# Linear attention and a gated feed-forward: batch 0's k by two queues, batch 1 in nine-token layout, batch 2's x copied by VectorE

## The chip, the core and the metric

The kernel runs on one core of a Trainium2 chip. A core has a matrix engine (TensorE, PE in the profile, with its weight loads as PEld), a vector engine (VectorE, DVE), an engine for activation functions (ScalarE, ACT), GpSimd (POOL) and SyncE (SP). Each works through its own queue of instructions in program order and waits on semaphores for the others. Matmul results go to PSUM, everything else lies in SBUF; transfers to and from memory run on 16 DMA engines and are started from the queues of POOL, SP or ACT. The metric is the time of one execution in microseconds, lower is better.

## What is computed

Eight batches of 576 tokens with 8 heads of 64 values go through linear attention with the feature map elu(x) + 1, and the result, as 4608 tokens of 512 values, through a feed-forward with a gated activation:

```python
def phi(x):
    return np.where(x > 0, x, np.exp(x) - 1.0) + 1.0
q_p, k_p = (phi(q), phi(k))
kv = np.einsum('bhsd,bhse->bhde', k_p, v)
z = np.sum(k_p, axis=2)
num = np.einsum('bhsd,bhde->bhse', q_p, kv)
den = np.einsum('bhsd,bhd->bhs', q_p, z)[..., None] + 1e-06
...
h = x @ w_in                                # 512 -> 2048
g = h * (1.0 / (1.0 + np.exp(-beta * h)))
return (g @ w_out).astype(np.float32)       # 2048 -> 512
```

## The kernel before, in words

**Stages.** For each batch the kernel computes phi of k and q, the product of k and v (`kv_mm`, with a column of ones beside v that gives z), the transposed q, the numerator and denominator (`num_mm`), their quotient x (`num_norm`), x transposed (`x_trans`), then h (`h_phase`, line 453, 64 matmuls of 512 columns) with the Silu on ACT (line 445), and y (`y_mm`, line 505, again 64 matmuls). The order is written out by hand: the attention of batch b+1 is woven between the matmuls of h and y of batch b through a plan, which says after which group of matmuls which pieces are issued. Every engine keeps exactly this order. The main work takes 512 tokens of each batch; the last 64 tokens of every batch (the "tail") are gathered in `xT_tail` and go through h and y together at the end.

**Two layouts of tokens.** Batches 1 to 7 put four tokens on each of 128 partitions and the 64 tail tokens in a fifth slot on half of the partitions; a load is one DMA of 1024 packets and one of 512 for the tail (lines 71 to 79). The unused half of the fifth slot has to be cleared by memsets (`clear_tail`, line 92). Batch 0 has a layout of its own: nine tokens on each of 64 partitions, with heads 0 to 3 on the lower half and heads 4 to 7 on the upper half (`nine`, `load_nine`, lines 117 to 138). It has no unused half and no tail load. Its token order follows it through to the stores of y (`store`, line 484 onwards).

**Start.** While batch 0's k, q and v come in, PE runs warm-up matmuls (`warm`, line 575). All loads of inputs go through POOL's queue, which casts fp32 to bf16 on the way: k, part of q, v in two parts, the rest of q, w_in, then half of w_out, k and q of batch 1. No more than eight of its DMAs are seen outstanding: POOL waits for the landing of an older one before it issues the next. beta, 8 KB, is issued by SP (line 147), turned by a matmul (`beta_trans`, line 193), and made ready by five small DVE operations (`make_beta`, lines 199 to 205). exp runs on ACT (line 256), max(x,0)+1 on DVE ("relu", line 264), and phi is the minimum of both (line 270). For batch 0 the matmuls for z and those for v are separate (`kv_mm0`, line 307), as v comes last.

**Batch 1** is prepared during h and y of batch 0: exp at line 229, relu at 237, phi at 242, the copy of v into `vaug` beside its ones (`v_copy`, line 370), then inside `y_phase_wide(0, ...)` the 40 matmuls of `kv_mm` (line 344), their four copies out of PSUM into `kv_bd` (line 355), the scaling of w_out by 1/beta (`w_out_scale`, line 212), 16 transposes of q (line 380), and `num_mm` (399) with `num_norm` (413 to 415) for one tile of 128 tokens after another. Matmul results of attention use two double banks of PSUM (`att_banks`), which take turns.

**Batch 2** has its q transposed by a DMA (line 388), and its x by PE (`x_trans`, line 433), with the copy out of PSUM on ACT (line 372) inside `y_phase_wide(1, ...)`.

Of the kernel before, what the change touches and what calls it, by code (L numbers as in the profile page):

```python
# [16 lines left out]
def kernel(  # L17
# [99 lines left out]
    def nine(a, spec):  # L117

        names = " ".join(spec)
        flat = a.rearrange("p a b c -> p (a b c)")  # L120
        size = {"h": HH, "j": N9, "d": D}
        n = size["h"] * size["j"] * size["d"]
        return flat[:, 0:n].rearrange(f"p ({names}) -> p {names}", **size)

    q9 = nine(xqk[0][:, 0], "hjd")
    k9 = nine(xqk[0][:, 1], "hjd")
    v9 = nine(vraw[0], "hjd")

    def load_nine(dst, src, h0=0, h1=HH, j0=0, j1=N9):
        for g in range(2):  # L130
            nc.gpsimd.dma_start(  # L131
                out=dst[g * TAIL : (g + 1) * TAIL, h0:h1, j0:j1, :].rearrange(
                    "p h j d -> p h (j d)"
                ),
                in_=src[0, g * HH + h0 : g * HH + h1, :, :]
                .rearrange("h (p j) d -> p h j d", j=N9)[:, :, j0:j1, :]
                .rearrange("p h j d -> p h (j d)"),
            )
# [5 lines left out]
    clear_tail(1)  # L144
    nc.vector.memset(vraw[1][TAIL:P, :, NJ, :], 0.0)
    beta_row = consts.tile([FC, P], F32)
    nc.sync.dma_start(out=beta_row, in_=moe_beta.rearrange("(c p) -> c p", p=P))
# [3 lines left out]
    load_nine(k9, k)  # L151
    load_nine(q9, q, j1=4)
    make_identity(nc, identity)
    make_identity(nc, ident16)
    load_nine(v9, v, j1=6)
    load_nine(v9, v, j0=6)
    load_nine(q9, q, j0=4)
# [4 lines left out]
    load_k(1)  # L162
    load_q(1)
# [15 lines left out]
    for i in range(2):  # L179
        set_ones(i)  # L180
# [67 lines left out]
    x0 = {0: q9, 1: k9}  # L248
# [4 lines left out]
    def exp0(a, j0, j1):  # L253
        if j0 == 0:
            st["e0", a] = work9("e", bufs=3)
        nc.scalar.activation(  # L256
            st["e0", a][:, j0:j1].rearrange("p j h d -> p h j d"), x0[a][:, :, j0:j1],
            ACTF.Exp,
        )

    def relu0(a, j0, j1):
        if j0 == 0:
            st["r0", a] = work9("r")
        nc.vector.tensor_scalar(
            st["r0", a][:, j0:j1].rearrange("p j h d -> p h j d"), x0[a][:, :, j0:j1],
            0.0, 1.0, ALU.max, ALU.add,
        )

    def phi0(a, j0, j1):
        nc.vector.tensor_tensor(  # L270
            st["p0"][a][:, j0:j1], st["r0", a][:, j0:j1], st["e0", a][:, j0:j1], ALU.min
        )

    def q_trans0(t, banks, c0):


        for jj in range(2 if t < NJ else 1):
            for a in range(2):
                for g in range(2):
                    gs = slice(g * TAIL, (g + 1) * TAIL)  # L280
                    m0 = c0 + a * P + jj * TAIL
                    nc.tensor.matmul(
                        banks[:, g, m0 : m0 + TAIL],
                        st["p0"][0][gs, 2 * t + jj, 2 * a : 2 * a + 2, :],
                        identity[gs, gs],
                        is_transpose=True, start=True, stop=True, skip_group_check=True,
                    )

    def q_out0(t, banks, c0, dve):
        n = rows(t)  # L290
        src = banks[:, :, c0 : c0 + 2 * P].rearrange("p g (a n) -> p g a n", a=2)
        dst = st[0, "qT"][:, t].rearrange("p (g a) n -> p g a n", g=2)
        copy(dst[:, :, :, :n], src[:, :, :, :n], dve)
# [5 lines left out]
    def kv_mm0(kvp, j0, j1, of_v):  # L299


        for j in range(j0, j1):
            for a in range(2):
                for g in range(2):
                    gs = slice(g * TAIL, (g + 1) * TAIL)
                    cols = kv_cols(kvp, g, a)
                    nc.tensor.matmul(
                        cols[:, :, 0:D] if of_v else cols[:, :, D],
                        st["p0"][1][gs, j, 2 * a : 2 * a + 2, :],
                        v9[gs, 2 * a : 2 * a + 2, j, :] if of_v else ones[gs],  # L310
                        start=(j == 0 and a == 0 and not of_v),
                        stop=(j == N9 - 1 and a == 1 and of_v),
                        skip_group_check=True,
                    )

    def kv_evac0(kvp):
        for g in range(2):
            for i in range(2):
                gs = slice(i * D, (i + 1) * D)
                copy(  # L320
                    kv_bd[0][g][gs, :, i, :],
                    kvp[g][gs, 0 : 4 * (D + 1)].rearrange(
                        "p (a i e) -> p a i e", a=2, i=2
                    )[:, :, i, :],
                    g == 0,
                )

# [153 lines left out]
    out0 = out[0:S, :].rearrange("(p j) m -> p j m", j=N9)  # L481

    def tail_rows(b):
        if b == 0:
            return out0[:, N9 - 1, :]
        return out[b * S + MAIN : (b + 1) * S, :]

    def store(b, t, y_sb):
        if b < B:
            if b == 0:  # L490
                for i in range(2):
                    nc.sync.dma_start(
                        out=out0[:, 2 * t + i, :], in_=y_sb[i * TAIL : (i + 1) * TAIL, :]
# [89 lines left out]
    def F(f, *a, **k):  # L583
        return lambda: f(*a, **k)

    begin(0)
    st["warm"] = mm_bank([P, 512])
    warm(10)
    beta_trans()
    make_beta()  # L590
    warm(20)
    st["p0"] = [
        nine(st[0, "p"][:, a].rearrange("p j (h d) -> p j h d", h=H), "jhd")
        for a in range(2)
    ]
    exp0(1, 0, 5)
    exp0(1, 5, N9)
    exp0(0, 0, 4)
    relu0(1, 0, 5)
    relu0(1, 5, N9)  # L600
    phi0(1, 0, 5)
    relu0(0, 0, 4)
    phi0(1, 5, N9)
    phi0(0, 0, 4)
# [3 lines left out]
    q_trans0(0, qb, 0)  # L608
    q_trans0(1, qb, 256)
    q_out0(0, qb, 0, False)  # L610
    q_out0(1, qb, 256, False)
    kv_mm0(kvp, 0, 6, True)
    kv_mm0(kvp, 6, N9, True)
    kv_evac0(kvp)
# [4 lines left out]
    exp0(0, 4, N9)  # L619
    relu0(0, 4, N9)  # L620
    silu_table()
    num_norm(0, 0)
    phi0(0, 4, 6)
# [3 lines left out]
    q_trans0(2, qb2, 0)  # L627
    q_out0(2, qb2, 0, False)
    num_norm(0, 1)
    phi0(0, 6, N9)  # L630
# [3 lines left out]
    load_v(1)  # L634
    load_w_out(3)

    def tidy0():
        clear_tail(0)
        nc.vector.memset(vraw[0][TAIL:P, :, NJ, :], 0.0)

    def q_rest0():
        q_trans0(3, qb2, 256)
        q_trans0(4, qb2, 512)
        q_out0(3, qb2, 256, False)
        q_out0(4, qb2, 512, False)
# [11 lines left out]
            9: [F(x_trans, 0, 3), F(tidy0)],  # L657
# [9 lines left out]
    begin(1)  # L667
    exp_(1, 1)
    exp_(1, 0)
    silu_table()  # L670
    relu(1, 1)
    relu(1, 0)
    w_out_scale(2)
    phi(1, 1)
    v_copy(1)
    phi(1, 0)
    y_phase_wide(0, {
        4: [F(load_next, 3)],
        9: [F(kv_mm, 1), F(kv_evac, 1), F(w_out_scale, 3)],
        10: [F(q_trans, 1, 0, 1, wide=True), F(q_trans, 1, 2, 3, wide=True)],  # L680
# [3 lines left out]
        14: [F(num_mm, 1, 3), F(num_norm, 1, 3), F(q_trans, 1, 4, wide=True)],  # L684
# [24 lines left out]
        12: [F(num_mm, 2, 1), F(num_norm, 2, 1), F(x_trans, 2, 0, wide=True)],  # L709
        13: [F(num_mm, 2, 2), F(num_norm, 2, 2), F(x_trans, 2, 1, wide=True)],  # L710
        14: [F(num_mm, 2, 3), F(num_norm, 2, 3)],
# [64 lines left out]
```

## Time and profile before

| | us |
|---|---|
| median of 8 runs (lowest, highest) | 296.24 (296.04, 297.16) |
| the profiled execution, as timed | 296.14 |
| its span, first to last instruction | 294.4 |
| PE busy | 285.6 (97%) |
| ACT busy | 175.1 (59%) |
| DVE busy | 123.8 (42%) |
| POOL busy | 53.1 (18%) |
| mean granted clock of TensorE | 0.998 |

How to read it: a row of the profile's timeline gives start, duration, engine, line of the kernel, operation, what it writes and reads with the shape, how many instructions are merged in it, and in brackets how long the engine stood idle before it and what released it. PE's busy time includes pipelined ends and the warm-up, so 97% does not say that PE works at its peak. The costliest groups are the matmuls of y (line 505, 128.2 us in 560 instructions) and of h (line 453, 108.1 us in 560, and 14.0 us for the tails); ACT's largest is the Silu (97.4 us). POOL's queue moved 20.45 MB in 38912 packets, the queues of SP and ACT 16.20 MB in 33216.

### The profile page before, as it was taken

To read this page: it belongs to the slowest core of one execution; us is meant where nothing else is said; L and a number is where in the kernel's file an instruction comes from. 1 tells how busy PE (TensorE), PEld (TensorE's weight loads), DVE (VectorE), ACT (ScalarE), POOL (GpSimd) and SP (SyncE) were. 2 spreads that over 40 slices of the span, in tenths; PEclk is the share of its full clock that TensorE was granted. 3 is DMA by queue.
4 is the path that set the end of the run, shared out by engine and by line. 5 is a ranking of instruction groups with operands and counts; after the bars stand their busy time and mean duration, and the time that the engine had idled before them with its cause. 6 is when DMAs were issued, how large, how long until landed. Compare 5 with 4: busy or idle time off the path is not lost.

```text
span 294.4 us, 4771 instructions
## 1 busy us (share of the span) xinstructions
PE 285.6 (97%) x1912; PEld 143.9 (49%) x1912; DVE 123.8 (42%) x261; ACT 175.1 (59%) x234; POOL 53.1 (18%) x72
## 2 busy tenths in 40 slices
PE   8979999999899999999999999999999999999994
PEld 2567445644465544454444544454445444444444
DVE  5675488504375264517461646164715400110012
ACT  2799776889988771878077808790770077018500
POOL 8924475540004200320032000000000000000000
PEclk9999999999999999999999999999999999999999
DMA  7999999999538993799369955023502400120032
GB/s 109 196 204 344 260 274 191 257 193 190 86 143 108 177 133 117 125 176 144 98 134 166 157 101 125 2 77 111 127 0 72 118 36 0 38 94 13 0 74 71
DMA packets 72310, 37.09 MB, mean 126 GB/s; under 512 B 40912, under 2 KB 66784, under 8 KB 72288
## 3 DMA queue, kind: packets, MB, share of 16 engines
q0 software_dynamic: 38912, 20.45, 47.9%
q1 hardware_dynamic: 33216, 16.20, 23.6%
q8 instruction: 15, 0.25, 0.3%
q10 hardware_dynamic: 160, 0.13, 0.2%
q14 instruction: 7, 0.06, 0.0%
HBM read 36.71 MB, written 9.44 MB: 157 GB/s over the span
## 4 chain that ended last, share of the span: by engine, by line
PE 77%; DMA 11%; ACT 4%; issue 3%; POOL 2%; DVE 1%; ACTq 0%; POOLq 0%; DVEq 0%
PE mm L453 37%; PE mm L505 34%; DMA vraw<-in_v_dram 6%; DMA xT<-in_moe_w_out_dram 5%; PE att L399 3%; ACT e L229 2%; PE att L344 1%; PE mm L537 1%; POOL xqk L131 1%; ACT L229 1%; ACT g L445 1%; DVE qk_p L242 1%; POOL xqk L111 0%; PE mm L433 0%; ACT L445 0%
## 5 line engine op out<-in xcount | busy, mean ns | idle before, releaser
L445 ACT ACTIVATE g<-mm,beta_c 128x512 bf16<-128x512 f32 (+2 forms) x156 | 97.4, 634 | 87.8 <-PE mm L453 87.5
L505 PE MATMUL mm<-w_out,g 128*128 128x512 bf16 x560 | 128.2, 379 | 0.0
L453 PE MATMUL mm<-xT,w_in 128*128 128x512 bf16 (+2 forms) x560 | 108.1, 349 | 0.8 <-DMA w_in<-in_moe_w_in_dram 0.5
L453 PEld LDWEIGHTS <-w_in 128*128 128x128 bf16 x656 | 62.0, 98 | 61.7 <-DMA w_in<-in_moe_w_in_dram 0.6
L505 PEld LDWEIGHTS <-g 128*128 128x128 bf16 x560 | 52.9, 98 | 58.3
L515 DVE COPY y_sb<-mm 128x512 f32<-128x512 f32 x27 | 18.7, 692 | 70.5 <-PE mm L505 69.1
L229 ACT ACTIVATE e<-xqk 128x2560 bf16<-128x2560 bf16 x14 | 31.9, 2329 | 0.1
L415 DVE TENSOR_TENSOR xs<-att,rden 128x512 bf16<-128x512 f32 (+1 forms) x40 | 27.6, 689 | 1.4
L242 DVE TENSOR_TENSOR qk_p<-r,e 128x2560 bf16<-128x2560 bf16 x14 | 20.9, 1490 | 13.1 <-ACT e L229 12.4
L72 POOL DMA_DIRECT2D vraw<-in_v_dram x7 | 7.0, 995 | 84.2 <-DVE vaug L370 78.4
L355 DVE CAST kv_bd<-att 64x130 bf16<-64x130 f32 x28 | 8.2, 292 | 32.2 <-PE att L344 31.8
L413 DVE TENSOR_SCALAR den<-att 128x8 f32<-128x8 f32 (+1 forms) x40 | 6.5, 162 | 31.4 <-PE att L399 31.3
L399 PEld LDWEIGHTS <-q_pT 128*128 128x128 bf16 (+1 forms) x160 | 11.6, 100 | 11.0 <-DVE xs L415 2.4
L399 PE MATMUL att<-kv_bd,q_pT 128*128 128x130 bf16 (+1 forms) x160 | 15.8, 221 | 1.1 <-DMA q_pT<-qk_p 0.7
L453 PE MATMUL mm<-xT_tail,w_in 128*128 128x512 bf16 x64 | 14.0, 379 | 0.0
L237 DVE TENSOR_SCALAR r<-xqk 128x2560 bf16<-128x2560 bf16 x14 | 11.6, 836 | 3.6 <-DMA xqk<-in_q_dram 2.2
L575 PE MATMUL mm<-g 128*128 128x512 bf16 x35 | 10.5, 457 | 1.2 <-DVE g L143 1.2
L72 POOL DMA_DIRECT2D xqk<-in_k_dram x7 | 9.4, 1336 | 5.7 <-DMA w_in<-in_moe_w_in_dram 2.2
L229 ACT ACT_TABLE_LOAD x7 | 9.0, 1283 | 0.1
L414 DVE RECIPROCAL rden<-den 128x8 f32<-128x8 f32 (+1 forms) x40 | 8.1, 202 | 1.4
L256 ACT ACTIVATE e<-xqk 128x1280 bf16<-128x1280 bf16 (+1 forms) x4 | 4.4, 1155 | 5.4 <-DMA xqk<-in_k_dram 4.6
L72 POOL DMA_DIRECT2D xqk<-in_q_dram x7 | 6.3, 894 | 5.5 <-ACT q_pT L372 1.9
(71 smaller groups left out, 138.5 us busy)
## 6 DMA issues: line engine op xcount, KB each, us to landing
out_dram<-y_sb SPq DMA_DIRECT2D x28, 256.0 KB, 2.3
xqk<-in_k_dram POOLq DMA_DIRECT2D x7, 512.0 KB, 10.7
xqk<-in_q_dram POOLq DMA_DIRECT2D x7, 512.0 KB, 11.6
vraw<-in_v_dram POOLq DMA_DIRECT2D x7, 512.0 KB, 11.3
w_in<-in_moe_w_in_dram POOLq DMA_DIRECT2D x4, 512.0 KB, 10.8
g<-in_moe_w_out_dram POOLq DMA_DIRECT2D x4, 512.0 KB, 10.9
out_dram<-y_sb SPq DMA_DIRECT2D x14, 128.0 KB, 5.2
xqk<-in_moe_w_out_dram POOLq DMA_DIRECT2D x2, 512.0 KB, 13.9
```

The lines of the kernel that those rows point to most:

```text
L72: eng.dma_start(out=dst[:, :, 0:NJ, :].rearrange("p h j d -> p h (j d)"), in_=src[b, :, 0:MAIN, :].rearrange("h (p j) d -> p h (j d)", j=NJ),)
L229: nc.scalar.activation(st[b, "e", a][:, h0:h1], xqk[b % NX][:, a, h0:h1], ACTF.Exp)
L237: nc.vector.tensor_scalar(st[b, "r", a][:, h0:h1], xqk[b % NX][:, a, h0:h1], 0.0, 1.0, ALU.max, ALU.add)
L242: nc.vector.tensor_tensor(st[b, "p"][:, a].rearrange("p j (h d) -> p h j d", h=H)[:, h0:h1], st[b, "r", a][:, h0:h1], st[b, "e", a][:, h0: ...
L355: nc.vector.tensor_copy(kv_bd[b % 2][i][gs, :, g, :], st[b, "kvp"][gs, 2 * i : 2 * i + 2, :])
L399: nc.tensor.matmul(nps[:n, p // 2, c0 : c0 + 2 * (D + 1)], st[b, "qT"][:, t, p, :n], kv_bd[b % 2][p // 2][:, p % 2], start=True, stop=True ...
L415: nc.vector.tensor_mul(xs[:n], nv[:, :, :, 0:D], rden[:n, :, :, None].to_broadcast([n, 2, 4, D]))
L445: nc.scalar.activation(g_sb[b % 2][:, ff, c0:c1], hp[:, c0:c1], ACTF.Silu, scale=beta_c[:, ff : ff + 1],)
L453: nc.tensor.matmul(hp[:, c0:c1], w_in_sb[ff // 4][:, kc, (ff % 4) * P : (ff % 4 + 1) * P], x[:, t0:t1, kc, :] if b < B else x[:, kc, c0:c1 ...
L505: nc.tensor.matmul(yp, g_sb[b % 2][:, ff, t * P : (t + 1) * P], w_out_sb[ff // 4][:, ff % 4, :], start=(ff == 0), stop=(ff == FC - 1),)
L515: nc.vector.tensor_copy(y_sb, yp)
L575: nc.tensor.matmul(st["warm"], g_sb[0][:, FC - 1, 0:P], g_sb[0][:, FC - 1, :], start=True, stop=True, skip_group_check=True,)
```

## The change

It touches three places.

1. **Start.** The last four of the nine token slots of batch 0's k (`k_last`) are no longer loaded by POOL as bf16 but by SP as fp32, into memory of `g_sb[1]` that is free then; POOL loads the first five. beta's load moves from SP to ACT's queue. `make_beta` moves behind batch 0's first phi operations, and the warm-up after `beta_trans` has 15 matmuls for 20. The copies of the first two transposed q tiles become one. The clearing of batch 1's tail leaves the start.
2. **Batch 1** takes the nine-token layout: its k, q and v are two DMAs each of 256 packets; exp, relu, phi and the copy of v use the layout's functions, now with a batch as argument (`exp9`, `relu9`, `phi9`, `q_trans9`, `q_out9`, `kv_evac9`). The product of k and v takes 36 matmuls on half of the rows each (`kv_mm9`), the transposed q 32 + 4 small ones. As later batches use the same buffers in the old layout, the halves of the fifth slot are cleared after batch 1's phi (`tidy(1)`), and the ones of `vaug` are set after its kv (`set_ones(1)`). Its stores follow the token order: two per tile, not one.
3. **Batch 2**: the copies of the first two x tiles out of PSUM are made by DVE, and the second of them comes one step later in the plan.

```diff
+    x9 = [[nine(xqk[b][:, a], "hjd") for a in range(2)] for b in range(2)]
+    v9 = [nine(vraw[b], "hjd") for b in range(2)]
+    va9 = nine(vaug[1], "jhd", EA)
+    QF = 4
+    KF = 5
+    k_last = g_f[:, 0 : HH * (N9 - KF) * D].rearrange(
+        "p (h j d) -> p h j d", h=HH, j=N9 - KF
+    )
+
+    def load_nine(dst, src, b, j0=0, j1=N9, eng=nc.gpsimd):
         for g in range(2):
+            eng.dma_start(
+                out=dst[g * TAIL : (g + 1) * TAIL].rearrange("p h j d -> p h (j d)"),
+                in_=src[b, g * HH : (g + 1) * HH, :, :]
...
-    clear_tail(1)
-    nc.vector.memset(vraw[1][TAIL:P, :, NJ, :], 0.0)
+    load_nine(k_last, k, 0, KF, N9, eng=nc.sync)
     beta_row = consts.tile([FC, P], F32)
-    nc.sync.dma_start(out=beta_row, in_=moe_beta.rearrange("(c p) -> c p", p=P))
+    nc.scalar.dma_start(out=beta_row, in_=moe_beta.rearrange("(c p) -> c p", p=P))
...
-    load_nine(k9, k)
-    load_nine(q9, q, j1=4)
+    load_nine(x9[0][1][:, :, 0:KF], k, 0, 0, KF)
+    load_nine(x9[0][0][:, :, 0:QF], q, 0, 0, QF)
...
-    load_k(1)
-    load_q(1)
+    load_nine(x9[1][1], k, 1)
+    load_nine(x9[1][0], q, 1)
...
-    for i in range(2):
-        set_ones(i)
+    set_ones(0)
+    nc.vector.memset(va9[:, :, :, D : D + 2], 1.0)
...
+    def in9(b, a, j0, j1):
+        if b == 0 and a == 1 and j0 >= KF:
+            return k_last[:, :, j0 - KF : j1 - KF]
+        return x9[b][a][:, :, j0:j1]
...
+    def kv_mm9(kvp):
+
+        for a in range(2):
+            for j in range(N9):
+                for g in range(2):
+                    gs = slice(g * TAIL, (g + 1) * TAIL)
+                    nc.tensor.matmul(
+                        kv_cols(kvp, g, a),
+                        st[1, "p9"][1][gs, j, 2 * a : 2 * a + 2, :],
+                        va9[gs, j, 2 * a : 2 * a + 2, 0 : D + 1],
+                        start=(j == 0), stop=(j == N9 - 1), skip_group_check=True,
+                    )
...
+    def v_copy9():
+        nc.vector.tensor_copy(
+            va9[:, :, :, 0:D].rearrange("p j h d -> p h j d"), v9[1]
+        )
...
     beta_trans()
+    warm(15)
+    exp9(0, 1, 0, KF)
+    exp9(0, 1, KF, N9)
+    exp9(0, 0, 0, QF)
+    relu9(0, 1, 0, KF)
+    relu9(0, 1, KF, N9)
+    phi9(0, 1, 0, KF)
+    relu9(0, 0, 0, QF)
+    phi9(0, 1, KF, N9)
+    phi9(0, 0, 0, QF)
     make_beta()
-    warm(20)
...
-    q_out0(0, qb, 0, False)
-    q_out0(1, qb, 256, False)
+    q_out9(0, 0, 2, qb, 0, False)
...
-    load_v(1)
+    load_nine(v9[1], v, 1)
...
-    phi(1, 1)
-    v_copy(1)
-    phi(1, 0)
+    phi9(1, 1)
+    v_copy9()
+    phi9(1, 0)
+    tidy(1)
+
+    def kv1():
+        kvp = att_banks()
+        kv_mm9([kvp[:, 0], kvp[:, 1]])
+        kv_evac9(1, [kvp[:, 0], kvp[:, 1]])
+        set_ones(1)
+
+    def q1():
+        qb = att_banks(BF16)
+        for t in range(NJ):
+            q_trans9(1, t, qb, 256 * t)
+        q_out9(1, 0, 1, qb, 0, False)
+        q_out9(1, 1, 2, qb, 256, False)
+        q_out9(1, 2, 4, qb, 512, False)
...
-        9: [F(kv_mm, 1), F(kv_evac, 1), F(w_out_scale, 3)],
-        10: [F(q_trans, 1, 0, 1, wide=True), F(q_trans, 1, 2, 3, wide=True)],
+        9: [F(kv1), F(w_out_scale, 3)],
+        10: [F(q1)],
...
-        12: [F(num_mm, 2, 1), F(num_norm, 2, 1), F(x_trans, 2, 0, wide=True)],
-        13: [F(num_mm, 2, 2), F(num_norm, 2, 2), F(x_trans, 2, 1, wide=True)],
-        14: [F(num_mm, 2, 3), F(num_norm, 2, 3)],
+        12: [F(num_mm, 2, 1), F(num_norm, 2, 1), F(x_trans, 2, 0, wide=True, dve=True)],
+        13: [F(num_mm, 2, 2), F(num_norm, 2, 2)],
+        14: [
+            F(x_trans, 2, 1, wide=True, dve=True), F(num_mm, 2, 3), F(num_norm, 2, 3),
+        ],
```

## The prediction

> **What bounds the kernel now.** I read the page's slices first, then the chain of waits, then short windows, then the timeline at the three places that the change touches.
>
> ```profile
> PE   8979999999899999999999999999999999999994
> DMA  7999999999538993799369955023502400120032
> GB/s 109 196 204 344 260 274 191 257 193 190 86 143 108 177 133 117 125 176 144 98 134 166 157 101 125 2 77 111 127 0 72 118 36 0 38 94 13 0 74 71
> ```
>
> TensorE (PE) is busy nearly everywhere, but until the first h matmul it only warms up. The DMA row is full for ten slices (to 73 us). So two things can shorten the run: an earlier first h matmul, or fewer holes in PE afterwards. In the chain:
>
> ```profile
> 5.31 5.68 DMA vraw<-in_v_dram
> ...
> 30.04 11.52 DMA vraw<-in_v_dram
> ...
> 45.05 0.62 PE att L380 x8
> ```
>
> The start hangs on batch 0's loads, and the stage of batch 1 on its v. After 82.4 us the chain is PE alone, so a hole saved or made before then reaches the end in full.
>
> **A. Start: k by two queues.** The windows (us, busy time per engine, clock, DMA share, GB/s written) show where the DMAs stand idle:
>
> ```profile
> 1.50:2.00 0.50, 0.50 (x2) 0.15 (x1) 0.50 (x2) 0.50 (x1) 0.50 (x2) 1.00 0.06 14
> 2.25:2.50 0.25, 0.25 (x3) 0.01 (x1) 0.25 (x2) 0.00 (x0) 0.25 (x1) 1.00 0.00 0
> 2.75:3.00 0.25, 0.25 (x2) 0.09 (x1) 0.25 (x2) 0.00 (x0) 0.25 (x1) 1.00 0.93 74
> 3.75:4.00 0.25, 0.25 (x2) 0.15 (x1) 0.12 (x2) 0.00 (x0) 0.25 (x2) 1.00 1.29 217
> ```
>
> From 3.5 us they write some 195 GB/s, which is 390 GB/s of fp32 read. Before 2.55 us nothing flows but beta's 8 KB, at 1.5 to 2.0 us, though SP issued it at 0.75. And what ends the start is this:
>
> ```profile
> 13.90 0.58 DVE L264 TENSOR_SCALAR r<-xqk 128x1280 bf16<-128x1280 bf16 x1 [0.77 <-DMA xqk<-in_q_dram]
> 14.51 0.17 DVE L413 TENSOR_SCALAR den<-att 128x8 f32<-128x8 f32 x1
> ...
> 16.78 1.07 PE L453 MATMUL mm<-xT,w_in 128*128 128x128 bf16 x16 [0.46 <-DMA w_in<-in_moe_w_in_dram]
> ```
>
> VectorE (DVE) holds the first normalisation behind relu of q's rest, which waits for its DMA until 13.90; PE waits for w_in until 16.78. Both lie behind k and v in one first-in-first-out stream, so k's own earlier arrival gains nothing there: what counts is how much of the stream's bytes moves before POOL's loads flow. k_last is 4/9 of k's 1.18 MB, 0.52 MB. SP has nothing else to issue until 48.29, so k_last can flow from 1.6 us (as beta did). A 128-packet store occupies SP for 0.96 us and a 64-packet one for 0.68, so some 5 ns a packet; 2 x 256 packets take 2.6 us, about 200 GB/s. From 1.6 to 2.55 that is 0.19 MB, and in the ramp to 3.5 (where POOL's loads use under half of 390) 0.19 MB more: 0.38 MB / 390 GB/s = 1.0 us. Bounds: 0.3 (the packets come slower, or the ramp is the memory's) and 1.3 (all of k_last). **I take 0.8 us**, since the page's smaller stores land slowly in traffic (5.2 us for 128 KB).
>
> [...]
>
> The rest keeps pace. k(0:5) is only 0.65 MB of POOL's stream, so exp begins near 5.7 rather than 6.88; DVE then runs relu 0.58, relu of fp32 (0.48 as bf16 up to 0.97, twice the 512-element fp32 row of L212), phi 0.83, relu 0.47, phi 0.7 and 0.7: done by about 10. make_beta's five operations (1.1 us) now stand behind them and before kv_evac, which cannot come before v (10.99 - 0.8) plus its 36 matmuls (11.12 to 12.46, 1.34 us), so they are hidden; beta_c is first read at 17.21. Five warm matmuls fewer (5 x 0.216) end PE's warm-up at 9.1, before it is wanted. The merged q copy (1.02 against 2 x 0.55) ends before kv_evac. The two memsets of batch 1 taken out (0.48 + 0.27) lay where DVE idles later anyway (3.96 to 5.93).
>
> beta now goes by ScalarE (ACT), behind its table load: issue at 2.24, not 0.75. Alone it landed in 1.7 us (3.9); in traffic, by the 128 KB stores, up to 5.2 (7.5). PE asks at 5.6 and must then run 15 warm matmuls. At 7.5 the v part of kv would start at 11.7 and den at 14.3 instead of 13.7: +0.6. With 16 packets it is nearest to its own row: 0.
>
> **B. Batch 1 in nine-token layout.** The stage before:
>
> ```profile
> 41.65 0.83 DVE L370 COPY vaug<-vraw 128x2560 bf16<-128x2560 bf16 x1 [0.41 <-DMA vraw<-in_v_dram]
> 42.53 0.82 PE L344 MATMUL att<-vaug,qk_p 128*64 128x65 bf16 x40
> 45.05 0.62 PE L380 MATMUL att<-identity,qk_p 128*128 128x128 bf16 x8 [0.28 <-DVE kv_bd L355]
> 46.80 0.17 DVE L413 TENSOR_SCALAR den<-att 128x8 f32<-128x8 f32 x1
> 47.99 0.40 PE L433 MATMUL att<-identity,xs 128*128 128x128 bf16 x4
> ```
>
> PE: 40 kv matmuls took 0.76 (42.53 to 43.29); 36 of batch 0's kind take 1.34: +0.58. The 16 transposes of q took 1.35 (44.16 to 45.51) with their wait for a bank behind kv_evac; 32 small ones, by batch 0's 16 in 0.23, take 0.5, and the new bank use has no such wait: -0.85. PE alone would gain 0.3. But x_trans at 47.99 is released by DVE, and DVE's queue from v's landing is a straight line: before, v_copy 0.83, phi 1.49, evac 1.2, w_out_scale 1.67 and gaps, 5.15 from 41.65 to 46.80. After: v_copy 0.75 and phi 1.34 (9/10 each), **tidy 0.75** (memsets of 0.48 and 0.27), evac 1.2, **ones 0.19**, scale 1.67, gaps 0.1: 6.0. That is +0.85. Behind tidy wait kv_evac, w_out_scale(3) and every norm, and PE waits for those.
>
> Against it v lands sooner against PE: 3 x 512 packets for 3 x 1536. Loads with tails wrote 187 to 195 GB/s at 58 to 74 us; whole nine-token rows 196 to 210 at 4.0 to 5.5. 5% of 9.3 us (1.77 MB at 190) is 0.45; I take 0.3, as batch 0's smaller pieces ran at 188. **B = +0.5 us**, from +0.1 (DMA gives 0.7, and DVE's 0.41 idle is used) to +0.9 (gives nothing). exp gets shorter (2.33 to 2.1, twice), relu longer (0.83 to about 1.0); neither is last. Batch 1's stores are eight SP issues (5.48 for batch 0) for four (3.85); the last starts near 86, and SP's next work, a transpose, at 89.26. Two new orders have room: w_out(2) goes into k_last's place, but was issued at 25.68, long after k's relu; v(3) waits for tidy, but was issued at 50.13.
>
> **C. Batch 2.**
>
> ```profile
> 78.96 0.40 PE L399 MATMUL att<-kv_bd,q_pT 128*128 128x130 bf16 x4 [0.67 <-DMA q_pT<-qk_p]
> 81.74 0.59 ACT L372 ACTIVATE xT<-att 128x512 bf16<-128x512 bf16 x1
> 82.38 0.38 PE L433 MATMUL att<-identity,xs 128*128 128x128 bf16 x4 [0.29 <-ACT xT L372]
> ```
>
> The second x_trans waits for the first one's copy to leave its bank: PE stands from 81.91 to 82.38, 0.46. By DVE the copy (0.42) follows xs at 81.63, ends at 82.05, and x_trans now comes after four more y matmuls, at 82.78: no wait. But num(2,3) then meets a bank whose norm, pushed behind the copy, ends at 83.2: a hole of 0.2. h would start at 84.36, not 84.55: **-0.2** (from +0.2, if DVE's added 2 x 0.42 delays the norms more, to -0.46).
>
> The 0.67 hole before is a DMA transpose issued at 69.61 among loads that fill the DMAs until about 76. The loads end sooner by A and by B's packets (1.1), while PE is ahead by only 0.3 there. **-0.4**, between 0 and -0.67.
>
> **Sum:** -0.8 + 0.5 - 0.2 - 0.4 = -0.9 us. The profiled execution took 296.14 (span 294.4 and 1.7 around it), which makes 295.2; the median of all runs is 296.24, so 295.3.
>
> **Rivals.**
> - *The transfer is hidden anyway.* [...] Against: the empty windows. -0.2 + 0.6 (less help for v) - 0.3 = +0.1: 296.3. Chance 0.25.
> - *DVE's queue in batch 1 becomes the bound* (slower). tidy and ones put 0.94 ahead of the norms; PE's longer kv matmuls hold kv_evac too. It decides once v lands less than 0.2 sooner against PE: B = +0.9, the transposed q gains nothing, and a start of only -0.2: +0.7, 296.9. For: every instruction from v to den is back to back. Against: 0.41 of idle before v_copy. Chance 0.15.
> - *All covers hold*: k_last wholly hidden (-1.1), v early (+0.1), hole at 78.96 closed (-0.67), copies -0.3: -2.0, 294.3. Chance 0.12.
> - The forecast: 0.48.
>
> A measurement of this kernel can tell about 0.2% (0.6 us) from no change: faster means below 295.65. Faster 0.48 + 0.12 = 0.60, same 0.25, slower 0.15. The range, 294.3 to 296.8, takes in the bounds of A, B and C added unevenly; the forecast's own is 294.7 to 295.9.
>
> **What would show it.** A: DMA share well above 0.3 in 2 to 3 us; relu of q's rest near 13.1; first h matmul near 16.0. B: from v_copy to den about 6.0 us; no wait of the q transposes for kv_bd; x_trans released by DVE. C: the wait for q_pT below 0.4, none for an xT copy. I am wrong if the first h matmul stays at 16.6 or later, if PE waits for beta, or if the stage from kv to the first h matmul of batch 1 (9.3 us) grows by over 0.9.

## The result, and the profile after

The kernel after the change takes **299.75 us** in the median of 11 runs (297.75 to 300.97), beside 296.5 for the kernel before, measured again (32 runs). The ratio is put at 1.0099 with a 95% interval of 1.0082 to 1.0115 (that of the two medians is 1.011): slower by one per cent, where 0.3% faster was predicted, and outside the predicted range.

Set side by side, the same events of the two profiled executions say where the time went:

| event, us from the start | before | after | difference |
|---|---|---|---|
| first h matmul of batch 0 | 16.78 | 17.01 | +0.2 |
| first y matmul of batch 0 | 33.77 | 34.01 | +0.2 |
| v of batch 1 copied (start) | 41.65 | 44.71 | **+3.1** |
| kv of batch 1 (start) | 42.53 | 45.53 | +3.0 |
| first h matmul of batch 1 | 51.84 | 56.24 | +4.4 |
| first h matmul of batch 2 | 84.55 | 87.99 | +3.4 |
| span | 294.4 | 298.0 | +3.6 |

The start gained nothing; 4.2 us were lost between batch 0's first y matmul and batch 1's first h matmul, while batch 1 is prepared; batch 2 gave back 1.0.

The slices of the page after, with the clock row this time (tenths of full speed granted to TensorE):

```profile
PE   8889978999999999999999999999999999999994
PEclk9899997999999999999999999999999999999999
DMA  8999999999728994599359945024503400120032
GB/s 150 189 207 339 252 242 197 223 225 184 103 55 148 167 171 115 121 141 174 114 121 142 171 117 119 7 70 114 116 9 73 116 35 0 37 81 25 0 73 70
```

In the first slice the DMAs move more than before (150 GB/s for 109), as the change wants it. But PE has a new dip in the sixth and seventh slices (37.2 to 52.2 us), and the clock row, which was all 9 before, falls to 8 and 7 in the second and the seventh.

From the chain of waits (start, duration, what):

```profile
13.83 18.16 DMA xT<-in_moe_w_out_dram
32.28 12.34 DMA vraw<-in_v_dram
49.25 1.98 DVE w_out L214 x4
```

Before, batch 1's stage hung on v's DMA, which ended at 41.6; now its last step before the copy ends at 44.6, and ahead of it stands a load of w_out that took 18 us. Behind it the chain runs on DVE. The timeline at batch 1 (start, duration, engine, line, what it writes and reads; in brackets the idle time before it and its releaser):

```profile
44.71 0.76 DVE L362 COPY vaug<-vraw 128x2304 bf16<-128x2304 bf16 x1 [0.58 <-DMA vraw<-in_v_dram]
45.53 1.38 PE L342 MATMUL att<-vaug,qk_p 64*128 64x130 bf16 x36 [2.73 <-DVE vaug L362]
46.90 0.48 DVE L92 MEMSET xqk<- 64x512 uint32 x1 [0.16 <-issue]
47.39 0.27 DVE L674 MEMSET vraw<- 64x256 uint32 x1
47.67 1.21 DVE L408 CAST kv_bd<-att 64x130 bf16<-64x130 f32 x4
48.67 1.03 PE L295 MATMUL att<-identity,qk_p 64*128 64x64 bf16 x32
49.25 1.98 DVE L214 TENSOR_SCALAR w_out<-g,rbeta 128x512 bf16<-128x512 f32 x4
51.26 0.17 DVE L451 TENSOR_SCALAR den<-att 128x8 f32<-128x8 f32 x1
```

Two things stand here. PE, which before went into kv without a wait, stands 2.73 us for v. And from the copy of v to den DVE works in a straight line of 6.55 us (44.71 to 51.26), as the prediction had it in kind, with 6.0 in size. In batch 2 the second x transpose, at 86.36, has no wait left before it.

### The profile page after: what moved, and what is told of

Read it like the earlier page. It is cut to its first block, busy times and chain, and to the rows that moved or that the text cites. A ratio compares the mean times of both kernels' runs of the same rounds, so it can differ in the third digit from the quotient of the medians.

```text
span 298.0 us, 4800 instructions
## 1 busy us (share of the span) xinstructions
PE 287.1 (96%) x1919; PEld 144.7 (49%) x1919; DVE 123.6 (41%) x264; ACT 173.6 (58%) x232; POOL 49.1 (16%) x72
## 3 DMA queue, kind: packets, MB, share of 16 engines
q1 hardware_dynamic: 33792, 16.72, 24.1%
## 4 chain that ended last, share of the span: by engine, by line
PE 80%; DMA 10%; POOL 4%; DVE 3%; issue 1%; POOLq 0%; DVEq 0%
PE mm L545 36%; PE mm L491 36%; DMA xT<-in_moe_w_out_dram 6%; DMA vraw<-in_v_dram 4%; PE att L437 3%; PE att L382 2%; POOL xqk L136 1%; PE mm L577 1%; PE att L491 1%; POOL w_in L161 1%; POOL vraw L136 1%; DVE xs L453 1%; DVE w_out L214 1%; POOL xqk L111 0%; DVE qk_p L282 0%
## 5 line engine op out<-in xcount | busy, mean ns | idle before, releaser
L231 ACT ACTIVATE e<-xqk 128x2560 bf16<-128x2560 bf16 x12 | 27.4, 2329 | 0.1
L244 DVE TENSOR_TENSOR qk_p<-r,e 128x2560 bf16<-128x2560 bf16 x12 | 17.9, 1493 | 13.1 <-ACT e L231 12.4
L393 DVE CAST kv_bd<-att 64x130 bf16<-64x130 f32 x24 | 7.0, 292 | 32.1 <-PE att L382 31.8
L72 POOL DMA_DIRECT2D vraw<-in_v_dram x6 | 5.3, 882 | 83.1 <-DVE vaug L408 79.1
L268 ACT ACTIVATE e<-xqk 128x1280 bf16<-128x1280 bf16 (+2 forms) x5 | 7.7, 1563 | 5.1 <-DMA xqk<-in_k_dram 5.0
L410 ACT ACTIVATE q_pT<-att 128x512 bf16<-128x512 bf16 (+2 forms) x8 | 4.9, 658 | 8.8 <-PE att L295 8.8
L239 DVE TENSOR_SCALAR r<-xqk 128x2560 bf16<-128x2560 bf16 x12 | 9.7, 816 | 0.0
L491 PE MATMUL att<-xT,w_in 128*128 128x512 bf16 x32 | 7.2, 379 | 0.0
```

The costliest lines, as they stand in the source:

```text
L231: nc.scalar.activation(st[b, "e", a][:, h0:h1], xqk[b % NX][:, a, h0:h1], ACTF.Exp)
L239: nc.vector.tensor_scalar(st[b, "r", a][:, h0:h1], xqk[b % NX][:, a, h0:h1], 0.0, 1.0, ALU.max, ALU.add)
L244: nc.vector.tensor_tensor(st[b, "p"][:, a].rearrange("p j (h d) -> p h j d", h=H)[:, h0:h1], st[b, "r", a][:, h0:h1], st[b, "e", a][:, h0: ...
L268: nc.scalar.activation(st[b, "e", a][:, j0:j1].rearrange("p j h d -> p h j d"), in9(b, a, j0, j1), ACTF.Exp,)
L491: nc.tensor.matmul(hp[:, c0:c1], w_in_sb[ff // 4][:, kc, (ff % 4) * P : (ff % 4 + 1) * P], x[:, t0:t1, kc, :] if b < B else x[:, kc, c0:c1 ...
```

## The experiments

### One part at a time: the start, batch 1, batch 2

Three kernels have one of the three parts each. `a_only` is the kernel after with batch 1 and batch 2 as before; `c_only` the kernel before with this edit (and the order of the plan that goes with it); `b_only` the kernel after with the start and batch 2 as before.

```diff
-        12: [F(num_mm, 2, 1), F(num_norm, 2, 1), F(x_trans, 2, 0, wide=True)],
+        12: [F(num_mm, 2, 1), F(num_norm, 2, 1), F(x_trans, 2, 0, wide=True, dve=True)],
```

> Only the start is changed (k by two queues, beta by ACT, 15 warm-up matmuls, make_beta later, one q copy). Theory 1 (the start gains nothing because k in smaller packets moves no more source bytes, and a short idle of PE lets its clock fall): first h matmul at 16.9 to 17.2 us, granted clock 0.5 somewhere between 12 and 16 us, whole time 296.4 to 297.2. Rival (the start did gain and batch 1 ate it): first h matmul before 16.5, time below 296.0.

> Only batch 1 is changed to nine tokens. Theory 1 (the loss of the whole change is here: loads that fill only 64 partitions hold up w_out, v lands late, PE waits and then runs at half clock): kv of batch 1 starts near 45.3 us rather than 42.5, PE idles 2 to 3 us before it, clock 0.5 for 3 us after it, time 300 to 301. Rival (DVE's queue with tidy and ones is the bound): no PE idle before kv, v copied near 41.5, time 296.7 to 297.3.

> Only batch 2's x copies are moved to DVE. Theory 1: the wait for the copy's bank goes, and num(2,3) meets a short wait: 0.1 to 0.3 us gained, the wait for the transposed q (0.7 us) stays, time 295.9 to 296.2. Rival (the 1 us that this stage gains in the changed kernel is all by the copies): the wait for the transposed q shrinks here too, time 295.2 to 295.6.

| kernel | us, median | ratio to before, 95% interval |
|---|---|---|
| `a_only` | 296.27 | 0.9997 [0.9985, 1.0009] |
| `b_only` | 300.89 | 1.0152 [1.0132, 1.0173] |
| `c_only` | 296.51 | 0.9999 [0.9989, 1.0009] |

`b_only` came as its theory said. `a_only` came as neither: the first h matmul of its profile is at 16.27, with no half clock, and the time lies between the two forecasts. `c_only` missed both, with no gain at all.

The loss is batch 1's alone, and the other two do nothing alone. But with both of them the loss is smaller: `b_only` is 1.1 us above the kernel after. Its timeline shows where:

```profile
44.62 0.76 DVE L359 COPY vaug<-vraw 128x2304 bf16<-128x2304 bf16 x1 [0.64 <-DMA vraw<-in_v_dram]
45.44 1.61 PE L339 MATMUL att<-vaug,qk_p 64*128 64x130 bf16 x36 [2.92 <-DVE vaug L359]
...
86.69 0.38 PE L468 MATMUL att<-identity,xs 128*128 128x128 bf16 x4 [1.12 <-ACT xT L407]
```

Batch 1 runs as in the kernel after, so the start plays no part in its delay. In batch 2 PE waits 1.12 us for ACT's copy of x, which the third part takes off ACT. How much that is worth shows from batch 1's first h matmul to batch 2's, over all kernels of this document (those not yet named come below):

| batch 2's copies | us from batch 1's h to batch 2's |
|---|---|
| by ACT: `before`, `a_only`, `a_warm`, `b_only`, `halves`, `two_h`, `even_odd` | 32.71 to 32.77 |
| by DVE: `after`, `c_only`, `fill`, `one1`, `tidy_pool`, `best1`, `best2`, `a_one` | 31.74 to 31.85 |
| by DVE, but PE waits 0.71 us for the transposed q: `no_start` | 32.62 |

So the copies are worth 0.97 us, whatever the start and batch 1 are, provided that the transposed q is there. And without them the q gains nothing by coming in time: in `b_only`, `halves`, `two_h` and `even_odd` PE has no wait for q, and waits 1.1 us for ACT's copy. Each of the two waits hides the other. `c_only` fits that: its profile, of an execution with half clock at the start (from 17.14 us), reaches batch 1's h 1.6 us late and finds q landed. That its other executions wait for q, and so gain nothing, is likely but not shown.

Why does the start alone give nothing? In its profile the first h matmul is half a microsecond earlier, and then:

```profile
16.27 1.05 PE L493 MATMUL mm<-xT,w_in 128*128 128x128 bf16 x16 [0.29 <-DVE xT L410]
...
41.59 0.83 DVE L410 COPY vaug<-vraw 128x2560 bf16<-128x2560 bf16 x1 [0.41 <-DMA vraw<-in_v_dram]
42.48 0.82 PE L384 MATMUL att<-vaug,qk_p 128*64 128x65 bf16 x40 [0.27 <-DVE vaug L410]
...
79.40 0.40 PE L439 MATMUL att<-kv_bd,q_pT 128*128 128x130 bf16 x4 [1.16 <-DMA q_pT<-qk_p]
84.55 0.60 PE L493 MATMUL mm<-xT,w_in 128*128 128x256 bf16 x4
```

Batch 1's v is copied at 41.59 us, for 41.65 before: PE comes earlier (batch 0's first y at 33.41 for 33.77), v does not, kv now waits for it, and batch 1's h starts at 51.78 for 51.84. The gain is lost there. The wait for batch 2's transposed q is longer, 1.16 for 0.67, since that DMA lands later in this execution (79.35 for 78.92); the wait for ACT's copy is gone in return, and batch 2's h starts at 84.55, as before.

Nor is the half microsecond surely the start's. Kernels whose start is unchanged have the first h matmul at 16.13 (`two_h`), 16.39 (`halves`), 16.72 (`b_only`), 16.77 (`even_odd`), 16.78 (`before`, `no_start`) and 17.31 (`c_only`): one execution of each, and `a_only` lies among them.

### Does the fallen clock cost the time in batch 1?

In the kernel after, the clock is at half speed for 3.41 us from 46.41 on, after PE's wait for v. `fill` keeps PE at work in that wait:

```diff
+        for _ in range(13):
+            nc.tensor.matmul(
+                kvp[:, 0, :], w_in_sb[0][:, 0, 0:P], w_in_sb[0][:, 0, :],
+                start=True, stop=True, skip_group_check=True,
+            )
         kv_mm9([kvp[:, 0], kvp[:, 1]])
```

> The changed kernel with 13 matmuls more in PE's queue ahead of batch 1's kv, into the bank that kv then starts afresh, so that PE isn't idle while it waits for v. Theory 1 (of the 4.4 us lost in this stage some 1.4 are the half clock after the wait): clock 1.0 from 45 to 50 us, kv still starts near 45.5 us, time 298.0 to 298.6. Rival (the clock follows the wait but costs nothing, as DVE is behind anyway): time within 0.3 us of the changed kernel's 299.75.

It takes 299.65 us, 1.0126 [1.0086, 1.0166] of before: no better than the kernel after, as the rival said.

```profile
43.18 2.97 PE L717 MATMUL att<-w_in 128*128 128x512 bf16 x13
46.08 1.21 PE L342 MATMUL att<-vaug,qk_p 64*128 64x130 bf16 x36
50.95 0.17 DVE L451 TENSOR_SCALAR den<-att 128x8 f32<-128x8 f32 x1
```

The clock stays full there and the kv matmuls take 1.21 us for 1.38, but den comes only 0.3 us earlier. The test isn't clean: v was copied at 44.12 in this execution, and the added matmuls ran past that and held kv up to 46.08, so that DVE waited 0.27 us for it. The profile of the kernel after settles it. From v's copy to den DVE waits for PE nowhere (the rows above), so slower matmuls move nothing there; and from den to batch 1's h, 51.26 to 56.24, it takes 4.98 us, for 4.99 in `one1` below at full clock. The half clock follows the late v and costs nothing here.

### Why is v late? Loads by halves of the partitions

The nine-token layout loads each of batch 1's k, q and v by two DMAs, one for partitions 0 to 63 and one for 64 to 127. `halves` does only this to the kernel before, in the old layout:

```diff
     def load_rows(dst, src, b, eng=nc.gpsimd):
-        eng.dma_start(
-            out=dst[:, :, 0:NJ, :].rearrange("p h j d -> p h (j d)"),
-            in_=src[b, :, 0:MAIN, :].rearrange("h (p j) d -> p h (j d)", j=NJ),
-        )
+        main = src[b, :, 0:MAIN, :].rearrange("h (p j) d -> p h (j d)", j=NJ)
+        for g in range(2 if b == 1 else 1):
+            ps = slice(g * 64, (g + 1) * 64) if b == 1 else slice(0, P)
+            eng.dma_start(
+                out=dst[ps, :, 0:NJ, :].rearrange("p h j d -> p h (j d)"), in_=main[ps]
+            )
```

`one1` is the kernel after with the opposite edit: each of batch 1's loads is one DMA over all 128 partitions. For that the even heads go to the lower half and the odd heads to the upper, so that the source is one regular pattern, and the quotient x is written in that order.

```diff
+    def load_one(dst, src, b, j0=0, j1=N9):
+        nc.gpsimd.dma_start(
+            out=dst.rearrange("p h j d -> p h (j d)"),
+            in_=src[b].rearrange("h s d -> (h s d)")
+            .rearrange("(r p c) -> p r c", p=P, c=N9 * D)[:, :, j0 * D : j1 * D],
+        )
...
-    load_nine(x9[1][1], k, 1)
-    load_nine(x9[1][0], q, 1)
+    load_one(x9[1][1], k, 1)
+    load_one(x9[1][0], q, 1)
...
-    load_nine(v9[1], v, 1)
+    load_one(v9[1], v, 1)
```

> The kernel before, with batch 1's loads of k, q and v in the old layout, their main part as two DMAs of 64 partitions each, with the same packets and bytes. [...] Rival (the larger packets of 1152 B hold up the others): v copied within 0.7 us of 41.65, time 296 to 297.

> The changed kernel with batch 1's k, q and v each as one DMA over all 128 partitions, even heads on the lower half and odd heads on the upper, the order put right where x is written. Packets and bytes are those of the changed kernel. Theory 1: w_out packets beside them take under 200 ns, v is copied by 41.5 us, PE doesn't wait for it, and what is left of the loss is DVE's queue (1.0 to 1.5 us): time 296.3 to 297.3. Rival (packets of 1152 B, not halves, slow w_out): v copied after 43.5, time above 298.5.

`halves` takes 300.98 us, 1.0153 [1.0116, 1.0191], the whole loss without the new layout: v is copied 3.7 us late, where the rival had at most 0.7. `one1` takes 296.21, 0.9985 [0.9973, 0.9997], so the layout without the halves loses nothing, and DVE's queue costs less than was expected. Batch 1 in `halves`:

```profile
45.36 0.83 DVE L372 COPY vaug<-vraw 128x2560 bf16<-128x2560 bf16 x1 [0.68 <-DMA vraw<-in_v_dram]
46.24 1.31 PE L346 MATMUL att<-vaug,qk_p 128*64 128x65 bf16 x40 [3.85 <-DVE vaug L372]
```

and in `one1`:

```profile
40.75 0.76 DVE L370 COPY vaug<-vraw 128x2304 bf16<-128x2304 bf16 x1 [0.59 <-DMA vraw<-in_v_dram]
42.35 1.21 PE L350 MATMUL att<-vaug,qk_p 64*128 64x130 bf16 x36
46.99 0.17 DVE L459 TENSOR_SCALAR den<-att 128x8 f32<-128x8 f32 x1
...
51.98 0.60 PE L504 MATMUL mm<-xT,w_in 128*128 128x256 bf16 x4
```

With whole loads v comes 0.9 us earlier than before (there is also one DMA for each load, so v's is issued sooner, at 25.59 for 28.74), and PE doesn't wait for it. From kv to batch 1's h it is 9.63 us, for 9.31 before: the layout's own price is 0.3.

Both kernels change two things at once, the partitions that one DMA writes and the number of DMAs. Two more kernels part them. `two_h` splits each main load by heads, with all partitions in each DMA; `even_odd` splits it into the even and the odd partitions:

```diff
+            hs = slice(g * 4, (g + 1) * 4) if b == 1 else slice(0, H)
+            eng.dma_start(
+                out=dst[:, hs, 0:NJ, :].rearrange("p h j d -> p h (j d)"),
+                in_=main[:, hs],
...
+            ps = slice(g, P, 2) if b == 1 else slice(0, P)
```

> The kernel before, with batch 1's three main loads each split into two DMAs by heads (heads 0 to 3, then 4 to 7): twice the DMAs, each over all 128 partitions, the same 1024 packets. Nothing is left out. Theory (a load that writes only one half of the partitions holds up the packets of w_out beside it): no half is written alone here, so v's copy starts within 0.6 us of 41.65, w_out packets keep a mean near 165 ns with under 20 of them over 250 ns, and the time stays within 0.3% of before (296.5). Rival (it is the number of DMAs: six instead of three take POOL's places for outstanding DMAs and its issue time): as with the halves of the partitions, v's copy at about 45 and 300 to 301 us.

> The kernel before, with batch 1's three main loads each split into two DMAs of 64 partitions, the even ones and the odd ones. Nothing is left out. [...] Rival (any DMA to 64 partitions, or twice the number of DMAs, does it): w_out packets 180 ns or more, v's copy at 44 to 45.5, time 300 to 301.

`two_h` takes 296.42 us, 0.9994 [0.9985, 1.0003]; `even_odd` takes 296.73, 1.0003 [0.9992, 1.0015]. So it is neither the number of DMAs nor 64 partitions as such: it is **the half**. In `even_odd` v's last DMA lands at 41.79 us, for 41.56 before:

```profile
41.91 1.26 DVE L372 COPY vaug<-vraw 128x2560 bf16<-128x2560 bf16 x1 [0.97 <-DMA vraw<-in_v_dram]
43.23 0.82 PE L346 MATMUL att<-vaug,qk_p 128*64 128x65 bf16 x40 [0.67 <-DVE vaug L372]
```

DVE's copy itself is longer here, 1.26 us for 0.83 (1.23 in `two_h`), and in these two executions batch 1's h comes 0.7 and 0.8 us later than in the profile of before; the medians show no such loss.

The trace also has each DMA packet with its size and duration. POOL's 4096-byte packets are those of w_out, fp32 over all partitions; half of w_out moves beside batch 1's loads:

```
kernel     w_out packets, mean ns   over 250 ns (of 1024)   last one starts, us   v copied, us
before              165                      5                    43.41              41.65
two_h               164                      7                    43.76              42.08
even_odd            167                      7                    43.62              41.91
one1                163                      5                    42.71              40.75
b_only              183                     91                    46.31              44.62
halves              197                    188                    47.04              45.36
after               198                    207                    46.38              44.71
```

The packets of k, q and v themselves hardly change: in `halves`, `two_h` and `even_odd` all write 512 bytes, in 62, 60 and 60 ns. What the loads to one half slow here is their neighbour: the w_out packets that start from 28 to 31 and from 38 to 43 us take 342 and 270 ns in `halves`, 168 and 167 in `even_odd`. So w_out lands late, and with it v. POOL's starts of v's loads come after waits of 0.58 and 1.73 us for older loads to land, here before and after, with what POOL waited for:

```profile
28.74 1.10 POOL L72 DMA_DIRECT2D vraw<-in_v_dram  x1 [0.58 <-DMA xT<-in_moe_w_out_dram]
...
32.28 0.77 POOL L136 DMA_DIRECT2D vraw<-in_v_dram  x1 [1.73 <-DMA xT<-in_moe_w_out_dram]
```

The third and fourth load of w_out landed at 28.45 and 29.75 us before; after, at 29.50 and 32.00 (`even_odd`: 28.61 and 29.91; `halves`: 29.22 and 32.20). v's second DMA, which ran from 30.04 for 11.52 us before, starts at 32.28 in the kernel after and takes 12.34: 2.2 us later and 0.8 longer, together the 3.1.

### Is DVE's queue in batch 1 the next bound?

`tidy_pool` is `one1` with tidy's memsets and the ones of `vaug` on GpSimd:

```diff
-    tidy(1)
+    nc.gpsimd.memset(xqk[1][TAIL:P, :, :, NJ, :], 0.0)
+    nc.gpsimd.memset(vraw[1][TAIL:P, :, NJ, :], 0.0)
...
-        set_ones(1)
+        nc.gpsimd.memset(vaug[1][:, :, :, D : D + 2], 1.0)
+        nc.gpsimd.memset(vaug[1][TAIL:P, NJ, :, D : D + 2], 0.0)
```

> The kernel of the one-DMA loads with the clearing after batch 1's phi and the ones after its kv made by GpSimd instead of DVE. Theory 1 (these memsets stand in the line from v to den): den of batch 1 comes 0.8 to 1.1 us sooner after v's copy, time 0.5 to 1.0 us below the kernel with one-DMA loads. Rival (the line is set by PE's longer kv matmuls, DVE would wait for them anyway): less than 0.3 us between the two.

It takes 295.94 us, 0.9975 [0.9965, 0.9985], 0.27 less than `one1` with intervals that overlap. Its profile fits the other theory:

```profile
44.04 1.21 DVE L416 CAST kv_bd<-att 64x130 bf16<-64x130 f32 x4 [1.46 <-PE att L350]
```

DVE, free of the memsets, waits 1.46 us for PE's kv. (PE's kv itself starts 0.44 us later in this execution than in that of `one1`, after a half clock at its start.) Once v is in time, the memsets lie in large part in a gap that PE leaves anyway; what moving them gives is not settled, and at most a few tenths.

### A version that beats both, and what the start is worth in it

`best1` joins what held: one DMA for each load of batches 0 and 1, the memsets on GpSimd, batch 2's copies by DVE, and the start's order as before.

> One-DMA loads for batch 0 and batch 1, the memsets by GpSimd, batch 2's copies by DVE, and the start as it was before the change (k by POOL alone, beta by SP, 20 warm-up matmuls). Theory 1 (with no half loads at all the DMA stream moves evenly, and fewer issues stand before v and w_in): first h matmul at 15.5 to 16.5 us, no half clock, time 294.3 to 295.8, faster than both kernels. Rival (the stream's bytes alone set it): first h matmul at 16.7 or later, time 295.8 to 296.6.

It takes **295.40 us**, 0.9962 [0.9951, 0.9973]: 0.4% under before and 1.5% under the kernel after. The time came as expected. The way to it can't be read from its profile, which is of the slowest of its 20 executions: 297.12 us at a granted clock of 0.991, where the other 19 took 295.27 to 295.99 at 0.997 or more. In that one the first h matmul is at 17.13, after 1.47 us of waiting for w_in, and the clock is at half speed from 17.19. Four kernels ask what warm-up and start are worth:

```diff
-    warm(15)
+    warm(24)
...
-    warm(4)
+    warm(8)
     x_trans(0, 0, dve=True)
```

`a_warm` is `a_only` with the first of these edits, `best2` is `best1` with the second. `no_start` is `tidy_pool` with the start as before the change. `a_one` is `tidy_pool` with the changed start, its loads by one DMA each, and both warm-ups.

> Only the start is changed, with 24 instead of 15 warm-up matmuls behind beta_trans, so that PE has no gap before k's first matmul. Theory 1 (the start's own gain in w_in's landing is about 0.5 us, and what reaches 79 us is taken up by the wait for the transposed q, whose DMA ends with the stream of loads): no half clock before 20 us, first h matmul 16.2 to 16.7, wait for q_pT at 79 us of 0.8 to 1.3 us, time 296.0 to 296.5, as before. Rival (the gain passes to the end): time 295.4 to 295.8, wait for q_pT no longer than the 0.67 us of before.

> One-DMA loads for batch 1, memsets by GpSimd, batch 2's copies by DVE, batch 0 loaded by halves and the start as before the change. Against the kernel that has the same and the changed start (295.94). Theory 1 (the changed start is worth nothing by itself: k comes 0.4 us later, w_in 0.5 us sooner, and PE's gaps bring half clock): within 0.4 us of 295.94. Rival (the start is worth the 0.8 us predicted): 296.6 to 296.9.

> The fastest kernel so far (295.40) with 8 warm-up matmuls instead of 4 in the gap while the first x is made. Theory 1 (a long gap of PE at 14.6 to 17 us let the clock fall to half in its profile): clock 1.0 at 17 to 21 us in the profile, time 294.6 to 295.2. Rival (PE waits for w_in there anyway): no change, 295.3 to 295.6.

> The one-DMA loads for both batches with the changed start on top: k's last four slots by SP as one DMA of fp32, beta by ACT, and 24 and 8 warm-up matmuls to keep PE busy. Theory 1 (smaller packets for k cost what the second queue brings): within 0.4 us of the same kernel without the changed start. Rival (the second queue gains once the clock holds): 0.6 to 1.0 us faster than it.

| kernel | us, median | ratio to before | first h matmul, us |
|---|---|---|---|
| `a_warm` | 296.22 | 0.9990 [0.9981, 0.9999] | 16.76 |
| `no_start` | 295.71 | 0.9976 [0.9967, 0.9984] | 16.78 |
| `best2` | 295.47 | 0.9967 [0.9954, 0.9979] | 16.86 |
| `a_one` | 295.63 | 0.9971 [0.9962, 0.9980] | 16.30 |

All four took the time that says nothing is gained. `a_warm` keeps the clock up and gives the start alone nothing: v is copied at 41.55, batch 1's h starts at 51.74, the wait for the transposed q is still there (0.86 us before 79.07), and batch 2's h starts at 84.46. `best2`, at full clock and with a wait for w_in of 0.79 us, takes what the ordinary executions of `best1` take; its first h matmul, at 16.86, is not in the 15.5 to 16.5 that were expected of `best1` either, so the reason given for that time isn't borne out. `a_one`'s profile has an early h, but is of its fastest execution (294.88). The intervals of the last three and of `best1` overlap: no gain from the order of the start can be measured here. The changed start with loads by halves and the clock kept up, on top of `tidy_pool`, was not run and stays open.

## Why the prediction was wrong, point by point

**Batch 1: the step that failed** is "Against it v lands sooner against PE: 3 x 512 packets for 3 x 1536 ... I take 0.3", with bounds of nothing and 0.7. v landed 3.1 us later. The step compared rates: tails against whole rows. The nine-token loads do run at the rate that was read for them (204 to 211 GB/s written at 30 to 33 us, in the kernel after and in `one1` alike). But those rates say nothing of the neighbour, whose packets took 198 ns in the mean in the one and 163 in the other, and no row of before shows nine-token halves beside w_out: in batch 0 they run beside each other and, for about a microsecond, w_in, whose packets keep their 98 to 100 ns there. What held is the direction for whole loads: in the six kernels that have them for batch 1, v is copied 0.1 to 1.2 us sooner than before. The bounds for a resource that the trace does not show excluded a loss, with no reason that excluded it.

**Batch 1: DVE's line** was predicted at 6.0 us from v's copy to den and took 6.55. The mechanism was right. Mis-sized were the scaling of w_out (1.98 us for the 1.67 that was taken over from before) and the gaps (about 0.35 for 0.1). PE's terms came near to what was worked out: 36 kv matmuls in 1.14 us at full clock (`one1`, 42.35 to 43.49) and 1.31 in the kernel after, where the clock falls on the way, for 1.34; the transposed q in 0.57 (`one1`; 0.96 in the kernel after, at half clock) for 0.5; and no wait for `kv_bd`. The rival that DVE's queue becomes the bound had the right sign and its place, but 3 of the 4.4 us at batch 1's h are v, and only some 1.4 are its.

**The start** was to bring h to 16.0; it came at 17.01 (16.27 in `a_only`). "k_last can flow from 1.6 us (as beta did)" was the first miss: beta's own packets moved at 1.78 to 2.09 before, and k_last's move from 2.27 to 5.77. Between 2 and 3 us the DMAs did fill, in the windows after (us, busy time per engine with number of instructions, clock, DMA share, GB/s written):

```profile
2.00:3.00 1.00, 1.00 (x4) 0.39 (x3) 0.56 (x6) 0.23 (x2) 1.00 (x3) 1.00 0.60 142
...
10.00:15.00 5.00, 3.99 (x79) 2.90 (x80) 3.88 (x13) 3.48 (x6) 4.40 (x7) 0.73 1.32 197
```

But exp of k started at 7.27 us, not 5.7. POOL's five slots of k move from 3.10 to 6.59, beside k_last, where all nine moved from 2.70 to 6.50 before: k as a whole is not sooner. So the rival "The transfer is hidden anyway", set aside for the empty windows, had the start right: `a_only` took 296.27 us, and 296.3 was its figure. The -0.2 for the start in its sum, and in that of the rival with DVE's queue, is shown by no run: in `a_only` the first h matmul came 0.5 us earlier than before, inside the 16.13 to 17.31 of the kernels with the start unchanged, and the whole time was 0.9997 of before. Loaded by one DMA each (`a_one`), k_last is through at 4.34 and exp starts at 6.45. beta, expected behind ACT's table load at 2.24, was issued at 0.92, and PE did not wait for it. "Five warm matmuls fewer ... before it is wanted" was costed at nothing; the warm-up's cover is gone by 9.1 us, PE has gaps, and the clock of the window from 10 to 15 us is 0.73. The last paragraph of this document says what that may cost.

**"A hole saved or made before then reaches the end in full"** failed by `a_only`: batch 1's v, 25 us after the first h, takes up what PE had gained, though the prediction itself names v as what that stage hangs on. The hole before the transposed q was to close by 0.4, as the loads end sooner. In the kernel after it closes because PE comes 3.4 us later; but in `one1`, `tidy_pool`, `best2` and `a_one`, where PE is at batch 1's h within half a microsecond of before, POOL's loads do end at 73.3 to 73.9 us, for 75.2, and q lands at 77.6 to 78.1, for 78.92: the reason that was given held there. In `no_start` it did not (75.2 and 78.95), and why is open.

**Batch 2's copies** did what was said: no wait for a copy of x is left. Predicted were 0.2 us for them and 0.4 for the hole before q. Alone they give nothing (0.9999); together with a q that is there they take 0.97 us off the stage, in eight kernels. The two terms were added as if each stood for itself, but while one wait is left the other gives nothing. That their sum, 0.6, comes near the 0.97 that was measured bears out neither of the two.

## What to carry to other kernels

A load split into two DMAs by halves of the partitions can keep its own rate and still delay a full-width load beside it (here 204 to 211 GB/s with and without the halves, and w_out's packets at 198 ns for 163): split by heads or alternate partitions (0.9994 and 1.0003 of before here, for 1.0153 by halves), or arrange the layout so that one DMA covers all 128 (0.9985). Bound a transfer's cost by what its neighbours lose as well as by its own rate, and let the bound reach below nothing where the trace has no such pair. Before crediting an early gain to the end, look for the next wait on something that doesn't move with it; here the v of the next batch, 25 us later, took it back. Where two waits stand in one stage, closing one can give nothing until the other is closed too (batch 2's copies: 0.9999 of before alone, 0.97 us off the stage with q landed). And before reading a profile, see whether its execution is an ordinary one of its kernel.

## What the runs showed of the hardware

**Halves.** The 4096-byte packets of a 128-partition load (w_out) take 342 and 270 ns in the mean of the two stretches beside loads to one half (`halves`), and 168 and 167 beside loads to even or odd partitions of the same packet size (`even_odd`). In the same stretches they take 330 and 251 ns in the kernel after and 168 and 163 in the kernel before. Why a half does this and every second partition does not is in no trace.

**The clock.** In the kernel after, PE's gaps of 0.33, 0.53 and 0.47 us between 9.1 and 11.2 us were followed by half clock from 12.28 on for 3.41 us, and its wait of 2.73 us for v by the same from 46.41 on. With 15 warm-up matmuls and the changed start the half clock of the start is in three of five profiles (`after`, `fill`, `tidy_pool`, and not in `a_only` and `one1`), with 24 in none of two. The granted clock of every execution says the same: 3.41 us at half speed in 294 us make a mean of 0.994 (an estimate from these two figures), and 31 of the 52 executions of `a_only`, `one1` and `tidy_pool` have 0.994 or less, none of the 36 of `a_warm` and `a_one`. Such executions took 1.0 us longer in the median in `one1` (11 at 296.60, the other 9 at 295.58) and 0.9 in `tidy_pool` (296.14 and 295.25), but only 0.2 in `a_only`, which fits v as its next limit. So the shortened warm-up, costed at nothing, likely costs up to 1 us where v is in time. Gaps of 1.3 us in three pieces, or of 2.73 in one, came before it here; its exact condition stays open.
